# Sketched linear attention and an FFN in one kernel: squares on GpSimd, a paired x step and a new hand-written order

## The chip, the cores and the metric

The kernel runs on one core of a Trainium2 chip. The metric is the device time of one execution in microseconds (us), lower is better. Engines: PE is TensorE (PEld its weight loads), DVE is VectorE, ACT is ScalarE, POOL is GpSimd, SP is SyncE, which here only issues DMAs.

## What is computed

Two layers in a row, batch 4, 4 heads of 32, 1088 positions, d_model 128, d_ff 1024, everything given and returned in float32:

```python
def phi(x):                       # S1, S2: 8 x 32
    a = einsum('rd,bhsd->bhsr', S1, x)
    b = einsum('rd,bhsd->bhsr', S2, x)
    return outer(a, b)            # 64 features
q_p, k_p = phi(q), phi(k)
kv  = einsum('bhsf,bhsd->bhfd', k_p, v);  z = sum(k_p, axis=2)
x   = einsum('bhsf,bhfd->bhsd', q_p, kv) / (einsum('bhsf,bhf->bhs', q_p, z) + 1e-6)
# heads side by side: x is (4, 1088, 128)
x_prev = x shifted by one position, zero first
k   = relu((mu_k * x + (1 - mu_k) * x_prev) @ w_k)
out = sigmoid((mu_r * x + (1 - mu_r) * x_prev) @ w_r) * ((k * k) @ w_v)
```

## The kernel before

The 4352 positions are 34 tiles of 128. The attention part goes through them in ten groups of 2 or 4 tiles (QS), the FFN in ten groups of 1 to 4 (FS); k is done batch by batch, each in two groups of 4 and 5 tiles (KG). Loads come in on SP's DMA queue in the order k, v, q of batch 0, 1, 2, 3; the FFN weights come on POOL's queue, cast to bf16 on the way.

Each piece of work is a task with a name, and one long string, ORDER, gives the order in which the tasks are issued and the engine of each, `NAME/ENGINE`, for PE tasks also the PSUM bank (b0 to b7) that they open. There is no other scheduler: an engine does its tasks in that order and waits by semaphores for what they need. The names, with the number of the batch (K and XL, XF, XE) or the group behind them:

- KT transposes k (DVE), KP projects it with S1 and S2 (PE, into PSUM), KE copies the projections to SBUF, KF forms the 64 products per head (DVE, `outer`), KA accumulates k features times v and the sums needed for z (PE). KZ, KC, KD, KW, KB turn these into the block that q is multiplied with: KW puts the z part into SW, the joint projection weight, KB puts kv into kvS.
- QT transposes q, Q1 projects it with S1, S2 and z (PE), QE copies the z part w to SBUF, QP, QD, QI, QN compute the denominator, its reciprocal and the normalised factor (DVE), QF forms the products (DVE), QR transposes them (PE), QV copies them to SBUF, QX multiplies with kv (PE: the x step, in array tiles of 64 x 32, one per head).
- XP, XB, XL, XK (and XF, XE on POOL) make the two mixes of x and its shift in bf16; the last 32 and the first 32 positions of a batch take the way over XL.
- M1 is the first FFN matmul of one 128-wide chunk of d_ff, RE its ReLU out of PSUM, SQ the square of two chunks at once (SBUF to SBUF, bf16), M2 the second matmul, which accumulates over four SQ. RR and SG are the gate, FN multiplies by it and issues the output DMAs on SP's queue, four per group, or eight where the group crosses a batch.
- Z runs dummy matmuls on a tile of zeros.

In the order before, squares go to DVE (27) and ACT (13), ReLUs to ACT (66) and DVE (14), all 20 QV to ACT. POOL has the setup, the weight DMAs, XF and XE.

The helper `copy` is line 302 (ACT) and 304 (DVE) of the profile, `outer` is line 316, the x step 500, M1 541, ReLU 549 (ACT) and 551 (DVE), squares 558 (DVE) and 560 (ACT), M2 570, FN 595 and its DMAs 605, the q projection 440, the POOL pieces 526 to 533, the dummies 246.

Of the kernel before, what the change touches and what calls it, by code (L numbers as in the profile page):

```python
# [33 lines left out]
KF1_1_0/DVE QV1_1/ACT QX0/PE/b3 QV1_0/ACT QX1/PE/b4 XB0/ACT XL0/ACT XP0/ACT QD2/DVE XF0/POOL KA1_1_0/PE QT1_1/DVE
XP1/ACT XB1/ACT RR0/PE/b2 RR1/PE/b0 XK0/DVE SG0/ACT XK1/DVE SG1/ACT M10_4/PE/b3 M10_6/PE/b2 M10_1/PE/b5 M10_3/PE/b6
KZ1/DVE RE0_4/ACT QI2/DVE M10_7/PE/b0 M11_3/PE/b4 RE0_6/ACT KT2_1/DVE KC1/ACT M10_2/PE/b3 RE0_3/ACT RE1_3/ACT
KD1/PE/b7 RE0_2/ACT QN2/DVE RE0_1/ACT SQ0_1/DVE M11_6/PE/b3 M11_2/PE/b5 QF2_1/DVE KP2_1/PE/b4 KB1/ACT RE1_2/ACT
RE0_7/DVE M11_0/PE/b6 SQ1_1/ACT KW1/DVE M11_1/PE/b5 RE1_6/DVE M11_7/PE/b2 Q14/PE/b7 KE2_1/ACT SQ0_3/DVE QF2_0/DVE
RE1_7/ACT RE1_0/ACT M10_0/PE/b4 M10_5/PE/b3 Q13/PE/b0 KF2_1_0/DVE RE1_1/ACT RE0_5/ACT RE0_0/ACT SQ1_0/ACT QR2_0/PE/b3
QE3/ACT QR2_1/PE/b4 QE4/ACT SQ0_2/DVE QV2_0/ACT QP3/DVE M21_0/PE/b5 SQ0_0/DVE M21_1/PE QV2_1/ACT QD3/DVE M11_4/PE/b3  # L40
SQ1_3/DVE M11_5/PE/b6 M20_0/PE/b1 M20_1/PE RE1_4/ACT QI3/DVE M20_2/PE KT2_0/DVE M20_3/PE RE1_5/ACT QX2/PE/b4 SQ1_2/ACT
QN3/DVE FN0/DVE QF3_0/DVE KP2_0/PE/b6 XB2/ACT M21_2/PE QF3_1/DVE XP2/ACT M21_3/PE RR2/PE/b1 QP4/DVE KE2_0/ACT FN1/DVE
QR3_0/PE/b0 XK2/DVE SG2/ACT QR3_1/PE/b5 QV3_0/ACT QD4/DVE M12_6/PE/b4 KF2_0_0/DVE QV3_1/ACT M12_1/PE/b1 M12_0/PE/b0
M12_7/PE/b6 RE2_6/ACT QX3/PE/b5 RE2_0/ACT QI4/DVE QT2_1/DVE RE2_1/ACT M12_3/PE/b0 M12_2/PE/b4 XL1/ACT XP3/ACT QN4/DVE
KA2_0_0/PE/b1 XF1/POOL SQ2_0/DVE RE2_3/ACT M12_5/PE/b3 QF4_0/DVE XE0/POOL KA2_1_0/PE RE2_2/ACT QF4_1/DVE M22_0/PE/b0
RE2_5/ACT KZ2/DVE M12_4/PE/b4 XB3/ACT KT3_0/DVE QR4_1/PE/b7 RE2_4/ACT QR4_0/PE/b3 KC2/DVE KT3_1/DVE QV4_1/ACT
RR3/PE/b1 QV4_0/ACT KP3_0/PE/b4 SQ2_2/DVE SG3/ACT KP3_1/PE/b7 XK3/DVE SQ2_1/ACT QX4/PE/b1 KE3_1/DVE RE2_7/ACT
KE3_0/DVE M22_1/PE KF3_1_0/DVE XP4/ACT M22_2/PE SQ2_3/ACT M13_3/PE/b6 M13_0/PE/b4 M13_6/PE/b7 XK4/DVE KD2/PE/b5
# [665 lines left out]
```

## Time and profile before

| what | value |
|---|---|
| median of 3 runs | 100.59 us (99.74 to 100.81) |
| the profiled execution's own time | 99.74 us |
| its span in the trace | 97.9 us |
| DVE, ACT, POOL busy | 81%, 71%, 13% of the span |
| PE matmuls busy | 85% of the span |
| share of DMA queue q1 (SP) | 35.8% of 16 engines' span |

The trace is of one execution, and the time outside the span, some 1.9 us, is start and end. Successive instructions of an engine overlap a little in such a trace, so the mean of one is some 0.08 us longer than the distance to the next. In rows with `<-`, what stands behind it ended the idle time of the engine.

### The profile page before, as it was taken

To read this page: it belongs to the slowest core of one execution; us is meant where nothing else is said; L and a number is where in the kernel's file an instruction comes from. 1 tells how busy PE (TensorE), PEld (TensorE's weight loads), DVE (VectorE), ACT (ScalarE), POOL (GpSimd) and SP (SyncE) were. 2 spreads that over 40 slices of the span, in tenths; PEclk is the share of its full clock that TensorE was granted. 3 is DMA by queue.
4 is the path that set the end of the run, shared out by engine and by line. 5 is a ranking of instruction groups with operands and counts; after the bars stand their busy time and mean duration, and the time that the engine had idled before them with its cause. 6 is when DMAs were issued, how large, how long until landed. Compare 5 with 4: busy or idle time off the path is not lost.

```text
span 97.9 us, 3150 instructions
## 1 busy us (share of the span) xinstructions
PE 83.0 (85%) x1272; PEld 56.9 (58%) x1282; DVE 79.5 (81%) x184; ACT 69.8 (71%) x166; POOL 12.7 (13%) x44
## 2 busy tenths in 40 slices
PE   4997878993899999899999999999999979997100
PEld 1354557651668584885686876935588546766000
DVE  3189959997594989989999999997999989997200
ACT  3250023476667899999999996999999979997000
POOL 7280031020000002400000002200353001000000
PEclk9999999999859999999999999999999999999975
DMA  2799999999993012000022012022000241011351
GB/s 64 248 224 331 279 250 335 233 246 340 171 198 79 12 27 54 7 0 0 0 60 60 0 40 67 7 59 48 0 0 20 67 107 30 0 32 32 81 120 44
DMA packets 10063, 9.72 MB, mean 99 GB/s; under 512 B 2480, under 2 KB 8880, under 8 KB 10048
## 3 DMA queue, kind: packets, MB, share of 16 engines
q1 hardware_dynamic: 8528, 8.92, 35.8%
q0 software_dynamic: 1216, 0.59, 4.3%
q8 instruction: 10, 0.16, 0.7%
q14 instruction: 5, 0.04, 0.2%
q10 hardware_dynamic: 304, 0.00, 0.2%
HBM read 7.80 MB, written 2.23 MB: 102 GB/s over the span
## 4 chain that ended last, share of the span: by engine, by line
PE 60%; DMA 13%; ACT 9%; DVE 8%; issue 3%
PE ps_o L570 14%; DMA hdk<-in_k_dram 13%; PE ps_h L541 13%; PE ps_x L500 8%; PE ps_abw L440 6%; PE ps_qtp L485 6%; PE ps_kab L333 4%; PE ps_kv L361 3%; ACT k L549 3%; PE ps_r L582 3%; DVE kp L316 3%; ACT k L560 3%; PE ps_r L583 2%; ACT r L588 1%; DVE qp L316 1%
## 5 line engine op out<-in xcount | busy, mean ns | idle before, releaser
L549 ACT ACTIVATE k<-ps_h 128x512 bf16<-128x512 f32 (+3 forms) x66 | 31.7, 568 | 2.9 <-PE ps_h L541 2.7
L541 PE MATMUL ps_h<-XK,wk 128*128 128x512 bf16 (+3 forms) x72 | 19.1, 351 | 2.4 <-issue 2.0
L570 PE MATMUL ps_o<-wv,k 128*128 128x128 bf16 x272 | 19.0, 219 | 0.8 <-ACT k L560 0.6
L570 PEld LDWEIGHTS <-k 128*128 128x128 bf16 x272 | 16.5, 98 | 4.7 <-ACT k L549 0.8
L558 DVE TENSOR_TENSOR k<-k 128x1024 bf16<-128x1024 bf16 (+3 forms) x27 | 15.9, 606 | 2.8 <-ACT k L549 2.7
L560 ACT ACTIVATE k<-k 128x1024 bf16<-128x1024 bf16 (+2 forms) x13 | 12.1, 951 | 0.1
L316 DVE TENSOR_TENSOR qp<-an,ps_abw 128x512 f32<-128x512 f32 x17 | 11.2, 678 | 0.0
L316 DVE TENSOR_TENSOR kp<-ab 128x512 f32<-128x512 f32 (+3 forms) x10 | 10.9, 1111 | 0.1
L541 PEld LDWEIGHTS <-wk 128*128 128x128 bf16 x80 | 6.5, 98 | 6.7 <-issue 4.2
L302 ACT COPY qpT<-ps_qtp 128x512 f32<-128x512 f32 (+1 forms) x20 | 9.9, 538 | 0.6 <-PE ps_qtp L485 0.3
L485 PE MATMUL ps_qtp<-ident,qp 128*128 128x128 f32 x68 | 9.6, 277 | 0.2 <-DVE qp L316 0.2
L500 PE MATMUL ps_x<-qpT,kvS 64*32 64x512 f32 (+7 forms) x104 | 9.3, 451 | 0.1
L526 POOL TENSOR_SCALAR PP<-XL,omu_k 128x31 f32<-128x31 f32 x4 | 2.0, 497 | 51.2 <-ACT XL L302 51.2
L485 PEld LDWEIGHTS ps_qtp<-ident,qp 128*128 128x128 f32 x68 | 7.5, 140 | 1.5 <-DVE qp L316 0.5
L551 DVE TENSOR_SCALAR k<-ps_h 128x512 bf16<-128x512 f32 (+3 forms) x14 | 8.3, 608 | 0.1
L440 PE MATMUL ps_abw<-SW,qT 128*64 128x96 f32 x136 | 8.3, 266 | 0.0
L246 PE MATMUL wt<-zero 128*128 128x512 bf16 x19 | 6.9, 515 | 1.6 <-DVE warm L155 1.2
L440 PEld LDWEIGHTS ps_abw<-SW,qT 128*64 128x64 f32 x136 | 6.6, 147 | 2.3 <-DVE pw L456 0.6
L595 DVE TENSOR_TENSOR osb<-ps_o,r 128x512 f32<-128x512 f32 (+3 forms) x10 | 6.0, 602 | 1.4 <-PE ps_o L570 1.4
L361 PE MATMUL ps_kv<-kp,vt 128*32 128x64 f32 x288 | 5.6, 222 | 1.6 <-DVE kp L316 1.2
L326 DVE STREAM_TRANSPOSE kT<-hdk 128x256 f32<-128x256 f32 (+1 forms) x16 | 6.1, 427 | 1.1 <-DMA hdk<-in_k_dram 1.0
L361 PEld LDWEIGHTS ps_kv<-kp,vt 128*32 128x32 f32 x288 | 4.5, 110 | 4.0 <-DVE kp L316 1.9
(77 smaller groups left out, 110.9 us busy)
## 6 DMA issues: line engine op xcount, KB each, us to landing
hdk<-in_k_dram SPq DMA_DIRECT2D x4, 544.0 KB, 10.0
hdq<-in_q_dram SPq DMA_DIRECT2D x4, 544.0 KB, 11.5
vt<-in_v_dram SPq DMA_DIRECT2D x4, 288.0 KB, 9.8
vt<-in_v_dram SPq DMA_DIRECT2D x4, 256.0 KB, 9.9
out_dram<-osb SPq DMA_DIRECT2D x16, 64.0 KB, 1.8
out_dram<-osb SPq DMA_DIRECT2D x20, 32.0 KB, 1.6
out_dram<-osb SPq DMA_DIRECT2D x8, 48.0 KB, 1.6
wk<-in_moe_w_k_dram POOLq DMA_DIRECT2D x1, 256.0 KB, 8.9
```

The lines of the kernel that those rows point to most:

```text
L302: nc.scalar.copy(o, i)
L316: nc.vector.tensor_mul(o.rearrange("p t h i j -> p (t h) i j"), _ap(a_, [[sa, y], [1, R], [0, R]]), _ap(b_, [[sb, y], [0, R], [1, R]]))
L361: nc.tensor.matmul(kv[32 * h:32 * h + 32, :64], vt[b][:, h, T, :], kp[:, t, h].rearrange("p i j -> p (i j)"), start=(T == 0), stop=(T == 8 ...
L440: nc.tensor.matmul(p[64 * c:64 * c + 64, t * 96:t * 96 + 96], qT[:, s:s + 64], SW[:, s // S].rearrange("p h x r -> p (h x r)"), skip_group ...
L485: nc.tensor.transpose(p[:, t * P:t * P + P], qp[g][:, t, 2 * pair:2 * pair + 2].rearrange("p h i j -> p (h i j)"), ident[:])
L500: nc.tensor.matmul(p[D * h:D * h + D, c0:c0 + m], kvS[r:r + 64, b, D * h:D * h + D], qpT[g][r:r + 64, h // 2, c0:c0 + m], skip_group_check ...
L541: nc.tensor.matmul(h[:, :n * P], wk[:, c * P:(c + 1) * P], XK[:, F0[g] * P:(F0[g] + n) * P])
L549: nc.scalar.activation(o, i, RELU)
L551: nc.vector.tensor_scalar(o, i, 0.0, None, op0=mybir.AluOpType.max)
L558: nc.vector.tensor_mul(k2[:, :, :n * P], k1[:, :, :n * P], k1[:, :, :n * P])
L560: nc.scalar.activation(k2[:, :, :n * P], k1[:, :, :n * P], mybir.ActivationFunctionType.Square)
L570: nc.tensor.matmul(o[:, t * P:t * P + P], k2s[g, j][:, c, t * P:t * P + P], wv[:, w * j + c, :], start=(j == 0 and c == 0 and t == 0), sto ...
```

## The change

The tasks stay the same in kind; their code, their engines and their order change.

- SQ goes to POOL (20) and ACT (17); only three squares of the last FFN group stay on DVE. ReLUs are now 55 on ACT and 25 on DVE, QV 14 and 6, QE 4 and 6, KE 6 and 2.
- KF reads one factor of the product straight from the PSUM bank of KP; the other still comes from the SBUF copy. The bank is therefore held until KF is done.
- QX is issued once for two groups (QY only opens the bank of the earlier one). For odd groups the heads of the features are rotated by one, by a copy of head 0 behind head 3 in SW, so that the two groups' eight matmuls stand in eight different array tiles.
- Q1 projects whole tiles of 128 positions, and splits only those that cross a batch.
- w_v is loaded with eight consecutive rows per partition, 4 KB in a run; the columns of w_k are permuted to match by a new task, WKP, on ACT. w_r is loaded on SP's queue behind q of batch 0 instead of POOL's.
- The zero tile is fp32 and the dummies are 3 at the start and 1 later, instead of 12 and 9.
- In ORDER, q of group 0 is now done before k of batch 1.

The diff without the ORDER string but for its first line, and without a task's cost figures, which nothing reads:

```diff
-KT0_0/DVE S4T/PE/b0 KT0_1/DVE S4E/ACT KP0_0/PE/b1 KE0_0/DVE KP0_1/PE/b0 KF0_0_1/DVE KE0_1/DVE KF0_0_0/DVE KF0_1_1/DVE
+KT0_0/DVE S4T/PE/b0 KT0_1/DVE S4E/ACT KP0_0/PE/b1 KE0_0/ACT KP0_1/PE/b0 KF0_0_1/DVE KE0_1/ACT KF0_0_0/DVE KF0_1_0/DVE
...
-    zero = const.tile([P, 512], BF16)
+    zero = const.tile([P, P], F32)
...
     load_q(0, nc.sync)
+    nc.sync.dma_start(wr_f[:], moe_w_r)
...
-    wk = const.tile([P, DFF], BF16)
+    wkn = const.tile([P, DFF], BF16)
+    wk = const.tile([P, NC, P], BF16)
...
-    nc.gpsimd.dma_start(wk[:], moe_w_k)
-    nc.gpsimd.dma_start(wr_f[:], moe_w_r)
-    nc.gpsimd.dma_start(wv[:], moe_w_v.rearrange("(c p) d -> p c d", p=P))
+    nc.gpsimd.dma_start(wkn[:], moe_w_k)
+    nc.gpsimd.dma_start(wv[:], moe_w_v.rearrange("(p c) d -> p c d", p=P))
...
-    SW = const.tile([FD, B, H, 3, R], F32)
+    SW = const.tile([FD, B, H + 1, 3, R], F32)
...
-            nc.tensor.matmul(wt[:], zero[:, :P], zero[:], skip_group_check=True)
+            nc.tensor.matmul(wt[:], zero[:], _ap(zero[:], [[0, 4], [1, P]]), skip_group_check=True)
 
-    dummy(12)
+    dummy(3)
...
+    nc.vector.tensor_copy(SW[:D, 0, H, :2, :], St[:, :, :R])
...
+    def wk_perm(eng):
+        o, i = wk[:].rearrange("p c f -> p f c"), wkn[:].rearrange("p (f c) -> p f c", c=NC)
+        if eng == "ACT":
+            nc.scalar.copy(o, i)
+        else:
+            nc.gpsimd.tensor_copy(o, i)
...
     def k_feat(b, gi, t0, t1):
-        a_, b_ = ab[:, 1, t0:t1], ab[:, 0, t0:t1]
-        outer(kp[:, t0:t1], a_, b_)
+        n = KG[gi][1] - KG[gi][0]
+        a_ = tiles[f"kab_{b}_{gi}"][:, :n * 64].rearrange("p (t h x r) -> p t h x r", h=H, x=2, r=R)[:, t0:t1, :, 1]
+        outer(kp[:, t0:t1], a_, ab[:, 0, t0:t1])
...
     def k_w(b, eng):
-        copy(eng, SW[:, b, :, 2, :], tiles[f"kf_{b}"][:, :HR].rearrange("p (h r) -> p h r", h=H))
+        w = tiles[f"kf_{b}"][:, :HR].rearrange("p (h r) -> p h r", h=H)
+        copy(eng, SW[:, b, :H, 2, :], w)
+        copy(eng, SW[:, b, H, 2, :], w[:, 0])
...
     def q_proj(g):
         p = bank(f"abw_{g}")
         for t in range(QS[g]):
-            for c in range(2):
-                s = (Q0[g] + t) * P + 64 * c
-                nc.tensor.matmul(p[64 * c:64 * c + 64, t * 96:t * 96 + 96], qT[:, s:s + 64],
-                                 SW[:, s // S].rearrange("p h x r -> p (h x r)"),
-                                 skip_group_check=True, tile_position=(0, 64 * c))
+            s = (Q0[g] + t) * P
+            whole = s // S == (s + P - 1) // S
+            for lo, hi in [(0, P)] if whole else [(0, 64), (64, P)]:
+                kw = {} if whole else dict(tile_position=(0, lo))
+                nc.tensor.matmul(p[lo:hi, t * 96:t * 96 + 96], qT[:, s + lo:s + hi],
+                                 SW[:, (s + lo) // S, g % 2:g % 2 + H].rearrange("p h x r -> p (h x r)"), skip_group_check=True, **kw)
...
-    def q_x(g):
-        p = bank(f"x_{g}")
-        for b, c0, s, m in qsegs(g):
-            for h in range(H):
-                r = 64 * (h % 2)
-                nc.tensor.matmul(p[D * h:D * h + D, c0:c0 + m], kvS[r:r + 64, b, D * h:D * h + D],
-                                 qpT[g][r:r + 64, h // 2, c0:c0 + m], skip_group_check=True, tile_position=(r, D * h))
+    def q_x(pair):
+
+        jobs = []
+        for i, g in enumerate(pair):
+            if i:
+                bank(f"x_{g}")
+            for n, (b, c0, s, m) in enumerate(qsegs(g)):
+                for y in range(H):
+                    h, r = (y + g % 2) % H, 64 * (y % 2)
+                    jobs.append((n, y, g, b, c0, m, h, r))
+        for n, y, g, b, c0, m, h, r in sorted(jobs):
+            nc.tensor.matmul(tiles[f"x_{g}"][D * h:D * h + D, c0:c0 + m], kvS[r:r + 64, b, D * h:D * h + D],
+                             qpT[g][r:r + 64, y // 2, c0:c0 + m], skip_group_check=True, tile_position=(r, D * h))
...
-    nc.tensor.matmul(h[:, :n * P], wk[:, c * P:(c + 1) * P], XK[:, F0[g] * P:(F0[g] + n) * P])
+    nc.tensor.matmul(h[:, :n * P], wk[:, c], XK[:, F0[g] * P:(F0[g] + n) * P])
...
     def sq(g, j, eng):
-        if eng == "DVE":
-            nc.vector.tensor_mul(k2[:, :, :n * P], k1[:, :, :n * P], k1[:, :, :n * P])
+        if eng != "ACT":
+            (nc.vector if eng == "DVE" else nc.gpsimd).tensor_mul(k2[:, :, :n * P], k1[:, :, :n * P], k1[:, :, :n * P])
```

How the new order moves instructions, at three places. A row is line, operation, output<-inputs and shape, in the order in which the engine does them. First the end of DVE: `k<-ps_h` is a ReLU, `k<-k` a square, `osb<-ps_o,r` is FN, here of the groups 7, 8 and 9. Before:

```order
L558 TENSOR_TENSOR k_1680<-k_1652 128x1024
L595 TENSOR_TENSOR osb<-ps_o,r 128x512
L558 TENSOR_TENSOR k_1711<-k_1630 128x1024
L558 TENSOR_TENSOR k_1721<-k_1687 128x1024
L551 TENSOR_SCALAR k_1723<-ps_h 128x384
L551 TENSOR_SCALAR k_1746<-ps_h 128x384
L551 TENSOR_SCALAR k_1717<-ps_h 128x384
L595 TENSOR_TENSOR osb<-ps_o,r 128x512
L558 TENSOR_TENSOR k_1775<-k_1717 128x2x384
L595 TENSOR_TENSOR osb<-ps_o,r 128x384
```

Now, also the end of DVE, with the last group's squares:

```order
L572 TENSOR_SCALAR k_1653<-ps_h 128x384
L572 TENSOR_SCALAR k_1631<-ps_h 128x384
L572 TENSOR_SCALAR k_1653<-ps_h 128x384
L579 TENSOR_TENSOR k_1685<-k_1639 128x2x384
L579 TENSOR_TENSOR k_1697<-k_1653 128x2x384
L616 TENSOR_TENSOR osb<-ps_o,r 128x512
L579 TENSOR_TENSOR k_1733<-k_1683 128x2x384
L616 TENSOR_TENSOR osb<-ps_o,r 128x512
L616 TENSOR_TENSOR osb<-ps_o,r 128x384
```

FN7 stood eight instructions ahead of FN9; it now stands three ahead of it, behind two of the last group's squares.

The end of POOL, XF and XE of the last batches, before (XL and PP are pieces of the x mix):

```order
L526 TENSOR_SCALAR PP<-XL,omu_k 128x31
L527 CAST XB<-XL 128x31
L528 CAST XB<-XL 128x32
L532 TENSOR_SCALAR XL<-XL,mu_k 128x32
L533 TENSOR_TENSOR XK<-XL,PP 128x32
L532 TENSOR_SCALAR XL<-XL,mu_k 128x32
L533 TENSOR_TENSOR XK<-XL,PP 128x32
```

Now, the same end of POOL:

```order
L579 TENSOR_TENSOR k_1398<-k_1221 128x1024
L579 TENSOR_TENSOR k_1453<-k_1363 128x1024
L579 TENSOR_TENSOR k_1513<-k_1449 128x1024
L579 TENSOR_TENSOR k_1540<-k_1468 128x1024
L553 TENSOR_SCALAR XL<-XL,mu_k 128x32
L554 TENSOR_TENSOR XK<-XL,PP 128x32
L579 TENSOR_TENSOR k_1606<-k_1580 128x1024
L579 TENSOR_TENSOR k_1651<-k_1608 128x1024
```

Full-size squares now stand in front of XE of the last batch and behind it, the last two being those of FFN group 8.

PE at the x step of the groups 0 and 1, before (ps_qtp are the transposes QR, ps_kv is KA; the numbers tell buffers apart):

```order
L485 MATMUL ps_qtp_386<-ident_110,qp_372 128x128 x2
L485 MATMUL ps_qtp_391<-ident_110,qp_372 128x128 x2
L500 MATMUL ps_x_398<-qpT_384,kvS_132 32x256 x4
L500 MATMUL ps_x_404<-qpT_396,kvS_132 32x256 x4
L361 MATMUL ps_kv_330<-kp_394,vt1_81 32x64 x20
```

Now, at the same step on PE, the first rows of eight that go on in turn:

```order
L500 MATMUL ps_qtp_348<-ident_112,qp_339 128x128 x2
L373 MATMUL ps_kv_356<-kp_341,vt1_81 32x64 x16
L379 MATMUL ps_kv_356<-ab_325 32x32 x4
L521 MATMUL ps_x_322<-qpT_310,kvS_134 32x256
L521 MATMUL ps_x_377<-qpT_351,kvS_134 32x256
```

The matmuls of two groups, into two PSUM banks, alternate where one group's four came after the other's.

More of the change, by code (lines that the diff above doesn't have):

```diff
@@ L34 @@
[L34 to L48, printed above, removed]
```

110 lines of the change are left out of this document (69 added, 41 removed).

## The prediction

> **What bounds the kernel now.** I read the busy times by stage first, cut where the kind of work changes, then who waits for whom, then the end of the program, the DMA queue included. By stage (busy us and, in brackets, instructions of each engine, then the granted clock, DMA share and GB/s):
>
> ```profile
> 0.00:4.60 4.60, 3.37 (x8) 1.16 (x9) 0.96 (x6) 1.49 (x2) 1.93 (x18) 1.00 0.51 154
> 4.60:24.00 19.40, 15.60 (x339) 10.31 (x340) 17.55 (x46) 7.35 (x30) 4.47 (x11) 1.00 1.10 280
> 24.00:34.00 10.00, 9.06 (x114) 6.61 (x115) 7.11 (x20) 6.92 (x20) 0.00 (x0) 0.83 0.66 120
> 34.00:84.00 50.00, 48.62 (x740) 34.04 (x745) 47.46 (x102) 48.00 (x104) 6.33 (x17) 1.00 0.14 32
> 84.00:91.54 7.54, 6.30 (x82) 4.80 (x80) 6.41 (x12) 6.04 (x12) 0.00 (x0) 1.00 0.13 29
> 91.54:97.90 6.36, 0.00 (x0) 0.00 (x0) 0.00 (x0) 0.00 (x0) 0.00 (x0) 0.72 0.35 84
> sum 97.90, PE 82.95 PEld 56.92 DVE 79.50 ACT 69.80 POOL 12.73; mean PE 13.82 PEld 9.49 DVE 13.25 ACT 11.63 POOL 2.12
> ```
>
> The reader is to see three things. From 34 to 84 us PE, DVE and ACT are all busy for 47 to 49 of 50 us, so taking work from one alone gives little there. DVE is full from the first k on: up to 91.54, where its last instruction ends, it works 79.5 us and idles 12.0 (3.6, 1.9, 2.9, 2.5 and 1.1 by stage). POOL idles. The 2.9 us between 24 and 34 have a cause of their own; the chain of waits and the list of waits show it:
>
> ```profile
> 23.60 1.34 issue
> ```
> ```profile
> PE ps_h L541 <- issue: 2.0, 1, 2.0
> DVE kT L326 <- DMA hdk<-in_k_dram: 1.0, 1, 1.0
> ```
>
> PE stands 2.0 us at the first FFN matmuls with nothing to wait for, and in the same stage its clock is 0.83. The end belongs to the queue that issues the output. Timeline of DVE, then two windows of SP:
>
> ```profile
> 85.62 0.68 DVE L595 TENSOR_TENSOR osb<-ps_o,r 128x512 f32<-128x512 f32 x1
> 88.84 0.68 DVE L595 TENSOR_TENSOR osb<-ps_o,r 128x512 f32<-128x512 f32 x1
> 89.44 0.55 DVE L558 TENSOR_TENSOR k<-k 128x768 bf16<-128x768 bf16 x1
> 90.98 0.56 DVE L595 TENSOR_TENSOR osb<-ps_o,r 128x384 f32<-128x384 f32 x1 [0.99 <-PE ps_o L570]
> ```
> ```profile
> 86.33 9.32 SPq L605 DMA_DIRECT2D out_dram<-osb  x16
> ```
> ```profile
> 91.63 1.82 SPq L605 DMA_DIRECT2D out_dram<-osb  x4
> ```
>
> FN7 ends at 86.30, and from 86.33 SP issues the 16 output DMAs of FN7 (8), FN8 (4) and FN9 (4) without a break until 95.65; FN9 has been done since 91.54. An issue costs 0.455 us undisturbed (1.82/4), 0.58 over the sixteen. The span ends 2.25 us after the last issue. So the end hangs on FN7 more than on FN9.
>
> **The change, part by part.** Rows by shape (busy us, then mean ns of one), the first four over all shapes:
>
> ```profile
> L549 ACT ACTIVATE k<-ps_h 128x512 bf16<-128x512 f32 (+3 forms) x66 | 31.7, 568 | 2.9 <-PE ps_h L541 2.7
> L558 DVE TENSOR_TENSOR k<-k 128x1024 bf16<-128x1024 bf16 (+3 forms) x27 | 15.9, 606 | 2.8 <-ACT k L549 2.7
> L560 ACT ACTIVATE k<-k 128x1024 bf16<-128x1024 bf16 (+2 forms) x13 | 12.1, 951 | 0.1
> L551 DVE TENSOR_SCALAR k<-ps_h 128x512 bf16<-128x512 f32 (+3 forms) x14 | 8.3, 608 | 0.1
> ```
> ```profile
> L302 ACT COPY qpT<-ps_qtp 128x512 f32<-128x512 f32 x14 | 8.0, 606 | 0.3
> L560 ACT ACTIVATE k<-k 128x1024 bf16<-128x1024 bf16 x7 | 7.5, 1075 | 0.0
> L316 DVE TENSOR_TENSOR qp<-an,ps_abw 128x512 f32<-128x512 f32 x17 | 11.2, 678 | 0.0
> L316 DVE TENSOR_TENSOR kp<-ab 128x512 f32<-128x512 f32 x3 | 2.0, 686 | 0.0
> L304 DVE CAST XB<-ps_x 128x512 bf16<-128x512 f32 x1 | 0.7, 692 | 0.6 <-ACT PP L509 0.6
> L304 DVE COPY ab<-ps_kab 128x256 f32<-128x256 f32 x3 | 1.3, 421 | 0.5 <-PE ps_kab L333 0.4
> L304 DVE COPY wsb<-ps_abw 128x128 f32<-128x128 f32 x1 | 0.3, 291 | 0.1
> ```
>
> *DVE.* Of 27 squares three of 768 columns stay: -(15.9 - 3 x 0.55) = -14.2. ReLUs rise from 14 to 25 and from 6144 to 11392 columns (counted in the two orders): +5248 x 8.3/6144 = +7.1. Six copies of transposed features come over: 5 x 0.69 + 0.42 = +3.9. Four more copies of w at 0.2 to 0.3: +1.0. Three k evacuations leave: -1.3. One XP, one small XB, three XL come, one KB goes, 0.2 to 0.75 each: +1.5. Sum -2.0 us, bounds -1.4 and -2.7 (successive DVE rows overlap by some 0.08 us, so any count is that uncertain per instruction).
>
> *ACT.* ReLU columns 28672 to 23424: -5.8. Squares 11008 to 15104 columns: +4.5. Six copies of features -3.4, four of w -1.0, k evacuations +1.2, the rest of the x step and k copies -0.8, the weight permutation +1.1 (the 1024-column row; its stride of 8 is not in the trace, bounds 0.9 and 2.2). Sum -4.2. The permutation waits for the w_k DMA and holds QE2 and QV0 behind it; the first FFN matmul that needs it comes some 8 us later. I take 0 on the path, 0.5 at most.
>
> *POOL.* It gets 20 squares, 17408 columns, 17 full-size ones. Rows of POOL, whole list, then one line's view with min/median/max, then a timeline of both engines:
>
> ```profile
> L532 POOL TENSOR_SCALAR XL<-XL,mu_k 128x32 f32<-128x32 f32 x4 | 1.5, 369 | 0.0
> L229 POOL TENSOR_SCALAR wr_c<-wr_f,mu_r 128x128 bf16<-128x128 f32 x1 | 0.6, 594 | 0.0
> ```
> ```profile
> L527 POOL CAST XB<-XL x4: 213/217/740, 21.0 to 70.5; 128x31 bf16<-128x31 f32 x4
> ```
> ```profile
> 70.50 1.30 DVE L558 TENSOR_TENSOR k<-k 128x1024 bf16<-128x1024 bf16 x2
> 70.51 0.74 POOL L527 CAST XB<-XL 128x31 bf16<-128x31 f32 x1
> 71.19 0.67 POOL L528 CAST XB<-XL 128x32 bf16<-128x32 f32 x1
> ```
>
> No POOL row is this wide. Lower bound: DVE's 0.68 us a square; upper: 369 ns for 32 columns in proportion, 11.8 us. The slope between the two POOL rows is (594-369)/96 = 2.34 ns a column, so 0.37 + 992 x 0.00234 = 2.7 us; I take that, as the slope is the nearest thing to a rate. POOL then has 17 x 2.7 + 6.3 (its work after 24) = 52 us, in about 60 us between the first ReLU pair and the last FFN output: off the path, though not by much. The Trainium skill, GPSIMD Engine Reference, section 3.1, states about 2.6 cycles an element for two inputs at 1.2 GHz, and section 4.1 advises VectorE for elementwise work as about twice as fast: an estimate of 2.2 us a square, and POOL at 44 us; no run here shows it yet.
>
> The casts that met DVE's squares took 0.74 and 0.67 us instead of 0.21, as long as the DVE square itself: a DVE instruction with both inputs in SBUF shuts POOL out. The k products were the other such kind (kp<-ab); reading one factor from PSUM costs nothing (678 against 686 ns) and keeps POOL free, at the price of a PSUM bank held about 1.2 us longer (0 to 0.5, taken as 0: there are eight).
>
> *PE.* Chain rows and the x group:
>
> ```profile
> 36.96 1.07 PE ps_x L500 x16
> 43.85 1.04 PE ps_x L500 x8
> 57.88 0.81 PE ps_abw L440 x16
> ```
> ```profile
> L500 PE MATMUL ps_x<-qpT,kvS 64*32 64x512 f32 (+7 forms) x104 | 9.3, 451 | 0.1
> ```
>
> A step of four array tiles takes 1.04 us for 512 columns; ten steps 9.3. If eight tiles run together, five steps cost 4 x 1.04 + 0.6 = 4.8: -4.5. If tiles in one column of the array take turns, 0; no row shows two such. I take -4, as the four tiles of today, two to a row half, overlap fully (eight 512-column passes in 1.04 us). The price is that the earlier group of a pair waits for the later. The q projection goes from 0.81/4 us a tile to two whole-array passes: 0 to -1, taken as 0.
>
> *At no cost.* The wr load is one more SP issue (64 KB, about 0.25 us at 280 GB/s) ahead of the next k; DVE now does q of group 0 before that k, which covers it and the old 1.0 us wait. wv in 4 KB runs lands earlier, but its first use is at 31 us. POOL issues one DMA fewer. Fewer and wider dummies: DVE sets the pace before 24 us (17.6 of 19.4), so 0; without that cover, a half-rate stretch like that of 24 to 34 us, 1.7 us. The k copies on ACT and KW0 on DVE add two waits of 0.4 to 0.7 us on DVE early, with the q work queued behind; they replace the 1.0 us wait for k: 0, bounds -1.0 and +1.2.
>
> *Sum.* DVE's last instruction: work -2.0. Idle at 24 to 34: the 2.9 falls to about 1.4, since the order there is another and half of it was PE's pause (bounds 0 and -2.9): -1.5. Idle after 34, 3.7 us: ACT and PE leave DVE waiting a little less: -0.8 (0 and -1.5). So FN9 ends 4.3 us earlier, at 87.2.
>
> The end, however, gets longer. On DVE FN7 now stands after the squares of the last group; between its end and FN9's are one square, FN8 and FN9: 0.55 + 0.68 + 0.56 = 1.8 us, where there were 5.2. All 16 issues follow FN7, so the span ends at FN9 - 1.8 + 16 x (0.455 to 0.58) + 2.25, that is 7.7 to 9.7 us behind FN9, where it was 6.36: +1.4 to +3.4. I take +2.0, nearer the undisturbed issue.
>
> Net -4.3 + 2.0 = -2.3 us. The profiled execution took 99.74 us, span 97.9; it was the fastest of three, 0.85 below the median of 100.59. The same step from the median: 98.3.
>
> **The rivals.** (A) The tail doesn't grow, because POOL or PE hands FN7 over in time or issues go at 0.455, and PE's pause at 24 us goes altogether: another -2.3, 96.0. For it: the pause waits for nothing that the profile names. Against: FN7's place in the order.
>
> (B) POOL shuts DVE out as DVE now shuts out POOL. At the very end POOL does its last two squares back to back just as DVE comes to its three squares from SBUF, ahead of FN7. If DVE must let the running one finish, some 1.6 us of 2.7, FN7 and all 16 issues shift: 99.9. The rows above show only POOL losing; POOL's pieces were too short to show the other. The Trainium skill, SBUF — State Buffer, section "Who interferes with whom", says that whoever issues first gets the shared pair for the whole instruction; its half that the rows show, they confirm.
>
> (C) Slower: POOL becomes the bound. It decides from (60 - 6.3)/17 = 3.2 us a square; each 0.1 us above adds 1.7. At 3.4 us POOL needs 64 us, FN9 ends 4.1 later: 102.4. For it: a two-input instruction may cost more than the one-input slope that I used, and XF, XE and the M2 groups queue behind squares in order. By the skill's estimate of 2.2 us, above, C would not happen.
>
> (D) The eight tiles take turns: the PE gain is gone, PE bounds 34 to 84 us as before, only the 1.5 us at 24 us stay, against a tail of +2.0: 101.1.
>
> **How the numbers follow.** Mine 0.42 (own range 97.0 to 99.8; 0.39 of it faster), A 0.17, B 0.20 (0.05 faster, 0.15 same), C 0.13, D 0.08 (0.06 same, 0.02 slower). About 1% is what a measurement of this kernel tells from no change. Faster 0.39 + 0.17 + 0.05 = 0.61; same 0.03 + 0.15 + 0.06 = 0.24; slower 0.13 + 0.02 = 0.15. The range leaves out most of C and the best part of A: 95.2 to 101.2.
>
> **What would show it.** POOL squares near 2.7 us (2.2 by the page; above 3.2 C). An x step over two groups near 1.04 us (2 us: D). DVE busy near 77.5 and done near 87. SP issuing 16 DMAs without a break from FN7 on, over 7.3 us long, and the span ending 8 us or so behind FN9 (6.4: A). A DVE square of the last group far over 0.55 us, or late beside a POOL square: B. Wrong altogether if DVE idles over 13 us: then the new order, and not the engines' sums, sets the time.

## The result, and the profile after

| | before | after |
|---|---|---|
| median of all runs (us) | 100.06 (48 runs) | 98.98 (43 runs) |
| profiled execution: own time, span (us) | 99.74, 97.9 | 98.58, 96.6 |
| FN7 ends, FN9 ends (us) | 86.30, 91.54 | 86.45, 88.10 |
| span end behind FN9 (us) | 6.36 | 8.50 |

The ratio after to before is 1.000, 95% interval 0.997 to 1.003: no difference that can be measured, where a gain of 2.3 us had been forecast. The ratio, like the medians in the table of experiments below, leaves out executions over 1.5% above the fastest of their kernel, and that matters here: of 59 runs of before beside the experiments the eleven with a granted clock (the mean share of full speed at which TensorE ran) of 0.975 or more have a median of 98.07 us, the 32 from 0.962 to 0.975 one of 99.78 and the 16 below one of 100.92, while the changed kernel shows 98.80 at 0.96 or more, 98.78 from 0.9425 to 0.96 and 99.42 below.

The changed kernel by stage, cut as before up to 84 us and then at the end of FN9 (busy us and instructions of PE, PEld, DVE, ACT, POOL, then clock, DMA share, GB/s):

```profile
0.00:4.60 4.60, 3.50 (x5) 1.61 (x6) 1.09 (x7) 1.49 (x2) 1.76 (x16) 1.00 0.55 152
4.60:24.00 19.40, 15.78 (x311) 11.63 (x309) 15.62 (x43) 11.38 (x25) 3.23 (x8) 0.82 1.03 279
24.00:34.00 10.00, 9.85 (x173) 8.11 (x172) 9.96 (x26) 8.48 (x29) 2.84 (x7) 1.00 0.57 129
34.00:84.00 50.00, 48.08 (x674) 34.87 (x665) 46.43 (x104) 45.92 (x92) 33.51 (x33) 1.00 0.15 31
84.00:88.10 4.10, 3.51 (x60) 3.18 (x57) 4.10 (x8) 2.28 (x5) 0.88 (x1) 1.00 0.08 16
88.10:96.60 8.50, 0.00 (x0) 0.00 (x0) 0.00 (x1) 0.00 (x0) 0.00 (x0) 0.77 0.38 78
sum 96.60, PE 80.72 PEld 59.41 DVE 77.20 ACT 69.55 POOL 42.22; mean PE 13.45 PEld 9.90 DVE 12.87 ACT 11.59 POOL 7.04
```

DVE works 77.2 us instead of 79.5, as forecast. Its idle time up to FN9 is 10.9 us instead of 12.0: 3.5, 3.8, 0.0, 3.6 and 0.0 by stage, where it was 3.6, 1.9, 2.9, 2.5 and 1.1. So the stage from 24 to 34 us gave 2.9, and the one before it took 1.9 back. The stretch in which TensorE runs at half its clock, here called the half rate, has moved too: the clock is 0.82 from 4.6 to 24 us and full from 24 to 34. Then the end, timeline of DVE and of SP:

```profile
84.82 1.03 DVE L579 TENSOR_TENSOR k<-k 128x768 bf16<-128x768 bf16 x2
85.76 0.69 DVE L616 TENSOR_TENSOR osb<-ps_o,r 128x512 f32<-128x512 f32 x1
86.38 0.56 DVE L579 TENSOR_TENSOR k<-k 128x768 bf16<-128x768 bf16 x1
86.86 1.24 DVE L616 TENSOR_TENSOR osb<-ps_o,r 128x512 f32<-128x512 f32 x2
```
```profile
86.48 7.75 SPq L626 DMA_DIRECT2D out_dram<-osb  x16
```

FN9 ends 3.4 us earlier, but FN7, which stands in front of all 16 last DMAs, ends where it did (86.45, was 86.30). SP then issues for 7.75 us without a break, 0.48 each. The prediction says the same of the profile before, but there the fourth of the 16 took 1.80 us, where all but one of the others took 0.3 to 0.45:

```profile
87.64 1.80 SPq L605 DMA_DIRECT2D out_dram<-osb  x1
```

With FN7 at the same place, that one issue is most of the 1.3 us by which the two spans differ (97.9 and 96.6). Rows that had been priced, by shape, and one step of the chain of waits:

```profile
L579 POOL TENSOR_TENSOR k<-k 128x1024 bf16<-128x1024 bf16 x16 | 30.1, 1892 | 12.3 <-ACT k L570 10.2 <-DVE k L572 1.9
L281 ACT COPY wk<-wkn 128x1024 bf16<-128x1024 bf16 x1 | 4.8, 4768 | 0.4 <-DMA wkn<-in_moe_w_k_dram 0.4
L456 PE MATMUL ps_abw<-SW,qT 128*128 128x96 f32 x64 | 9.5, 290 | 0.6 <-DVE SW L315 0.6
```
```profile
33.48 1.02 PE ps_x L521 x17
```

A POOL square takes 1.89 us, the permutation of w_k 4.77, an x step of two groups 1.02.

### The profile page after: what moved, and what is told of

It reads as the page before. It is cut to its first block, busy times and chain, and to the rows that moved or that the text cites. A ratio compares the mean times of both kernels' runs of the same rounds, so it can differ in the third digit from the quotient of the medians.

```text
span 96.6 us, 3021 instructions
## 1 busy us (share of the span) xinstructions
PE 80.7 (84%) x1199; PEld 59.4 (61%) x1205; DVE 77.2 (80%) x185; ACT 69.5 (72%) x151; POOL 42.2 (44%) x63
## 4 chain that ended last, share of the span: by engine, by line
PE 53%; DVE 18%; DMA 8%; ACT 5%; SPq 4%; issue 2%; ACTq 0%
PE ps_o L591 12%; PE ps_h L562 10%; DMA vt<-in_v_dram 7%; PE ps_qtp L500 6%; PE ps_abw L456 6%; PE ps_kv L373 5%; PE ps_kab L344 4%; PE ps_x L521 4%; DVE XK L534 4%; DVE kT L337 3%; DVE k L572 3%; SPq L626 3%; PE ps_r L603 2%; DVE qp L327 2%; DMA out_dram<-osb 1%
## 5 line engine op out<-in xcount | busy, mean ns | idle before, releaser
L579 POOL TENSOR_TENSOR k<-k 128x1024 bf16<-128x1024 bf16 (+1 forms) x20 | 32.5, 1636 | 14.6 <-ACT k L570 12.5
L570 ACT ACTIVATE k<-ps_h 128x512 bf16<-128x512 f32 (+3 forms) x55 | 25.7, 541 | 1.3 <-PE ps_h L562 1.1
L572 DVE TENSOR_SCALAR k<-ps_h 128x512 bf16<-128x512 f32 (+2 forms) x25 | 14.4, 623 | 0.1
L327 DVE TENSOR_TENSOR kp<-ps_kab,ab 128x512 f32<-128x512 f32 (+3 forms) x10 | 10.9, 1112 | 1.2 <-ACT ab L313 1.2
L456 PE MATMUL ps_abw<-SW,qT 128*128 128x96 f32 (+1 forms) x72 | 10.2, 288 | 0.6 <-DVE SW L315 0.6
L456 PEld LDWEIGHTS ps_abw<-SW,qT 128*128 128x128 f32 (+1 forms) x72 | 8.8, 191 | 2.1 <-DVE SW L315 0.8
L534 DVE SCALAR_TENSOR_TENSOR XK<-ps_x,mu_k,PP 128x512 bf16<-128x512 f32 (+8 forms) x13 | 6.7, 536 | 0.7 <-ACT XB L313 0.7
L344 PE MATMUL ps_kab<-SW,kT 128*64 128x64 f32 x144 | 6.7, 250 | 0.2 <-ACT qpT L313 0.2
L344 PEld LDWEIGHTS ps_kab<-SW,kT 128*64 128x64 f32 x144 | 5.6, 159 | 1.4 <-ACT qpT L313 0.4
L603 PE MATMUL ps_r<-wr_c,XB 128*128 128x128 bf16 (+1 forms) x36 | 5.3, 224 | 1.4 <-ACT XB L313 0.9
```

Source lines behind the costliest of these rows:

```text
L327: nc.vector.tensor_mul(o.rearrange("p t h i j -> p (t h) i j"), _ap(a_, [[sa, y], [1, R], [0, R]]), _ap(b_, [[sb, y], [0, R], [1, R]]))
L344: nc.tensor.matmul(p[64 * c:64 * c + 64, (t - t0) * 64:(t - t0) * 64 + 64], kT[b][:, t, 64 * c:64 * c + 64], SW[:, 0, :H, :2, :], skip_gro ...
L456: nc.tensor.matmul(p[lo:hi, t * 96:t * 96 + 96], qT[:, s + lo:s + hi], SW[:, (s + lo) // S, g % 2:g % 2 + H].rearrange("p h x r -> p (h x ...
L534: nc.vector.scalar_tensor_tensor(XK[:, b * S + s:b * S + s + m], tiles[f"x_{g}"][:, c0:c0 + m], mu_k[:], PP[:, b * XW + s:b * XW + s + m], ...
L570: nc.scalar.activation(o, i, RELU)
L572: nc.vector.tensor_scalar(o, i, 0.0, None, op0=mybir.AluOpType.max)
```

## The experiments

Three theories went in. *Queue*: the change did win time, but the end hangs on FN7 and the 16 issues behind it. *Start*: the gain is lost before 27 us. *Chance*: the profile of before held accidents. Each kernel is one edit of before, of after, or of an earlier experiment. They were measured in four groups of rows (four, four, four and three). The ratio is to runs of before taken with the group; that base moves (its median is 99.5, 98.0 and 99.3 us in the first three groups, and the kernel before against itself gave 0.986), so the kernels' own medians are the better guide from group to group. By the same median after has 98.78 us. The last three kernels have no ratio.

| kernel | median us (runs kept, of all) | ratio, 95% | FN7, FN9 end | span |
|---|---|---|---|---|
| before_again | 98.19 (2 of 4) | 0.986 (0.976 to 0.996) | 86.94, 92.17 | 98.2 |
| after_fn7 | 97.02 (4 of 6) | 0.975 (0.967 to 0.982) | 84.87, 88.87 | 95.1 |
| after_2q | 95.71 (4 of 6) | 0.960 (0.954 to 0.967) | 86.91, 88.56 | 93.8 |
| before_2q | 96.26 (3 of 6) | 0.967 (0.959 to 0.974) | 84.96, 90.20 | 93.8 |
| after_both | 95.12 (5 of 6) | 0.976 (0.966 to 0.985) | 84.55, 88.56 | 93.0 |
| both_x1 | 97.68 (6 of 10) | 0.999 (0.989 to 1.009) | 87.85, 91.86 | 96.3 |
| both_q64 | 97.00 (5 of 10) | 0.991 (0.984 to 0.998) | 86.22, 90.23 | 96.0 |
| b2q_pool | 108.16 (4 of 4) | 1.109 (1.095 to 1.124) | 95.98, 102.58 | 106.2 |
| both_wkpool | 94.87 (5 of 6) | 0.956 (0.950 to 0.963) | 85.01, 89.02 | 93.5 |
| both_wundo | 94.85 (5 of 6) | 0.957 (0.952 to 0.962) | 84.56, 88.57 | 93.1 |
| both_kpsb | 97.32 (4 of 4) | 0.981 (0.975 to 0.988) | 86.66, 90.66 | 95.2 |
| before_late3 | 96.14 (3 of 4) | 0.969 (0.962 to 0.975) | 87.30, 92.53 | 96.4 |
| wundo_ke | 95.04 (4 of 6) | | 84.69, 88.69 | 93.2 |
| both_dummies | 95.56 (6 of 6) | | 85.17, 89.17 | 93.6 |
| both_sqdve | 102.26 (4 of 4) | | 92.14, 96.14 | 100.6 |

**before_again.** No edit.

> The kernel before, unchanged. Three theories of why the changed kernel gained nothing. Queue: FN9 does end earlier (88.10 against 91.54 us in the two profiles), but the end hangs on FN7, which ends at 86.45 now and 86.30 before, followed by 16 output DMAs at 0.47 us each and 2.4 us. Start: the gain is lost before 27 us, where DVE now idles 3.7 instead of 1.9 us (5.6 and 4.6 to 24) and the FFN begins 4 us later. Chance: the first profile of before held stalls that other executions do not have (PE's pause of 2.0 us at 23.6, TensorE at half rate for 3.4 us, two breaks of 1.4 and 0.45 us in SP's issues after FN7). Queue expects FN7 to end within 0.5 us of 86.3 again and the span to end 16 x 0.47 + 2.4 = 9.9 us behind it (96.2) if no issue is broken. Chance expects DVE's idle time between 24 and 34 us to fall from 2.9 to 1.5 us or less, and FN7 at 85 or before. Start expects the idle time as it was, 12.0 us to FN9. The ratio to before must be 1.00.

DVE's busy time from 24 to 34 us is 6.54 us here, and 7.98 in before_2q, whose clock was full all the time (third column of busy times):

```profile
24.00:34.00 10.00, 8.37 (x100) 5.98 (x99) 6.54 (x19) 6.54 (x19) 0.00 (x0) 0.83 0.52 111
```
```profile
24.00:34.00 10.00, 8.92 (x135) 6.82 (x135) 7.98 (x23) 7.91 (x23) 0.00 (x0) 1.00 0.62 128
```

The idle time of DVE there is 3.5 us (2.9 in the first profile) and still 2.0 in before_2q, so this stall is no accident. FN7 ends 0.6 us later than in the first profile and SP's 16 issues took 8.7 us, again with a long one (1.23 us), so the span is 98.2 and not 96.2. PE's pause at the first FFN matmul is there every time: 2.0 us in the first profile, 2.6 in this one, 2.3 in before_2q. The half rate near 26 us is there in two of the three, and FN9 ends at 91.54 and 92.17 with it, at 90.20 without. Chance is right for the half rate alone.

**after_fn7.** FN7 and the matmuls that it needs, moved ahead:

```diff
-... RE9_3/DVE M28_0/PE/b3 RE9_5/DVE M28_1/PE RE9_1/ACT RE9_2/DVE M27_3/PE RE9_6/ACT
+... RE9_3/DVE M27_3/PE FN7/DVE M28_0/PE/b3 RE9_5/DVE M28_1/PE RE9_1/ACT RE9_2/DVE RE9_6/ACT
-... RE9_7/ACT FN7/DVE M28_3/PE
+... RE9_7/ACT M28_3/PE
```

> The changed kernel with M2 of FFN group 7's last piece and FN7 put some ten tasks earlier in the order; nothing else. POOL's last square of group 7 ends at 79.4 us, so FN7 can end near 83.2 instead of 86.45. Queue: FN7's 8 DMAs are then issued by 87, FN8 (87.5) and FN9 (88.15) follow without a queue in front of them, the last issue ends near 91.3, the span near 93.7: 2.9 us less than the changed kernel (ratio to before 0.97). Start and chance: the end follows FN9, which does not move: within 0.5 us of the changed kernel (ratio 0.995 to 1.005).

```profile
84.18 0.69 DVE L616 TENSOR_TENSOR osb<-ps_o,r 128x512 f32<-128x512 f32 x1 [0.21 <-PE ps_o L591]
```
```profile
84.90 7.83 SPq L626 DMA_DIRECT2D out_dram<-osb  x16
```

FN7 ends 1.6 us earlier, the span 1.5 us, although FN9 ends 0.8 us later than in after: the end follows FN7. By medians it is 1.8 us, less than the 2.9 expected: FN7 ends at 84.87, not at 83.2.

**after_2q and before_2q.** In after every second DMA of the groups 7 to 9 goes to ACT's queue; in before, where ACT still works behind FN7, those of FN8 and half of FN9's:

```diff
-                nc.sync.dma_start(orow[b][:, x:x + 4 * m - 3:4, :], o[32 * y:32 * y + 32, t:t + m, :])
+                eng = nc.scalar if g > 6 and y % 2 else nc.sync
+                eng.dma_start(orow[b][:, x:x + 4 * m - 3:4, :], o[32 * y:32 * y + 32, t:t + m, :])
```
```diff
+                eng = nc.scalar if g == 8 or g == 9 and y % 2 else nc.sync
+                eng.dma_start(orow[b][:, x:x + 4 * m - 3:4, :], o[32 * y:32 * y + 32, t:t + m, :])
...
-RE9_6/DVE FN8/DVE SQ9_2/ACT
+RE9_6/DVE SQ9_2/ACT FN8/DVE
```

> The changed kernel with every second output DMA of FN7, FN8 and FN9 issued on ACT's queue, which is done with its work at 86.3 us. Queue: eight issues on each queue from 86.5, done at 90.2, span end 92.6 instead of 96.6: 4 us less (ratio to before 0.96). If the moving of the bytes and not the issuing sets the end, nothing changes. Start and chance: under 1 us, since the issuing would not be what ate the gain.

> The kernel before with FN8's four output DMAs on ACT's queue (behind ACT's last square, 90.04 us) and FN9's four shared by both queues; FN7's eight stay on SP, since ACT still works then. Queue: the end hangs on FN9 here (91.54 + 0.94 + 2.3 = 94.8 to 95.1 us) instead of 96.2 to 97.9, a ratio of 0.97 to 0.99; and the changed kernel with two queues must be 2 to 2.5 us faster than this one, because with the queue out of the way FN9's 3.4 us show. Start and chance: the two kernels with two queues differ by under 1 us, as the two kernels with one do.

SP in after_2q, then in before_2q:

```profile
86.94 3.67 SPq L627 DMA_DIRECT2D out_dram<-osb  x8
```
```profile
84.99 6.04 SPq L606 DMA_DIRECT2D out_dram<-osb  x10
```

Both are some 3 us faster than their originals (98.78 to 95.71, and a ratio of 0.967): the issuing set the end in both. With one queue FN7 alone counts, and FN7 had not moved. But after_2q beats before_2q by 0.6 us, not by the 2 to 2.5 that Queue expected and within the 1 us that Start and Chance allowed: if the tail hid a gain, it was far smaller than thought. In after_2q all 16 issues still stand behind FN7, so the next kernel moves that too.

**after_both.** after_fn7 with FN8's DMAs and one of FN9's on ACT's queue (`g == 8 or g == 9 and y == 3`).

> The changed kernel with FN7 early (as in the run with FN7 alone moved) and both queues: FN7's eight DMAs on SP, FN8's four on ACT, FN9's four 3 to 1. Queue theory: FN7 ends near 84.9, its issues are through at 88.6, FN9 ends near 88.8, the last issue 1.4 us later and the span 2.4 after that: 92.6, so 1.2 us less than the changed kernel with two queues alone (93.8), ratio to before near 0.95. If the queue had no part left in the end: 93.8 again, 0.96. Full forecast: FN9 earlier by 4.3 us than in before would mean FN9 at 87.2 and 91.0 us; the profiles so far have it at 88.1 to 88.9, against 90.3 to 92.2 in before.

```profile
83.86 0.69 DVE L616 TENSOR_TENSOR osb<-ps_o,r 128x512 f32<-128x512 f32 x1 [0.21 <-PE ps_o L591]
88.00 0.56 DVE L616 TENSOR_TENSOR osb<-ps_o,r 128x384 f32<-128x384 f32 x1 [0.31 <-PE ps_o L591]
```
```profile
84.58 5.29 SPq L627 DMA_DIRECT2D out_dram<-osb  x11
```
```profile
87.72 2.39 ACTq L627 DMA_DIRECT2D out_dram<-osb  x5
```

The last issues, on SP and on ACT (second and third fence), are now FN9's, and the span ends 4.4 us behind FN9. 95.12 us is 3.7 less than after, and 1.1 less than before_2q, whose end is FN9's too. FN9 ends 1.6 us earlier than in before_2q, but its issue on ACT waits behind FN8's four, and the spans differ by 0.8 (93.0 and 93.8). So the change is worth 1.6 us at FN9 and 0.8 to 1.1 us of time where FN7 doesn't stand in front of it, against the 4.3 of the forecast at FN9.

**both_x1.** The x step one group at a time: `QY` becomes `QX` in the order, and

```diff
-        two = (g - 1, g) if g % 2 else (g,)
+        two = (g,)
```

> The kernel after_both with the x step undone: one group at a time, four matmuls in four array tiles, at the place in the order where the group's bank was opened; the heads stay rotated. If the eight tiles saved PE time on the path: PE busy rises by 4 us (x groups near 1.04 us for 512 columns each, ten instead of five) and the time by 1 to 4 us. If PE only waits less somewhere else: PE busy +4 us, time within 0.5 us, since DVE sets FN9. If the early bank and the wait for the later group cost more than the pair saves: 0.5 to 1 us faster.

The x step in the stretch from 0 to 90 us, both_x1 and then after_both (PE first):

```profile
0.00:90.00 90.00, 8.72 (x104) 2.04 (x104) 9.80 (x21) 8.51 (x22) 0.96 0.41 101
```
```profile
0.00:90.00 90.00, 5.03 (x104) 1.53 (x104) 9.87 (x21) 8.55 (x22) 1.00 0.43 105
```

3.7 us of PE, a little of it by the half rate that both_x1's profile had from 12.8 to 19.6 us, and 2.6 us of time: the eight tiles run together, and PE's time is on the path.

**both_q64.** The q projection in tiles of 64 positions again (`for lo, hi in [(0, 64), (64, P)]`).

> The kernel after_both with the q projection in tiles of 64 positions again (68 matmuls of 128 x 64 weights instead of whole ones). In the profiles a group of four took 0.81 us before and 1.02 to 1.06 now, 8 x 0.2 us of PE. If that is on the path, 0.5 to 1.6 us faster, and the first groups' waits of DVE for the projection (0.7 us before the copy of w) shrink by 0.2 us each; if DVE sets the pace, within 0.3 us of after_both, with PE busy 1.6 to 2 us less.

```profile
PE ps_abw L456 <- issue: 1.4, 1, 1.4
```

Slower by 1.9 us, against both expectations. PE's 705th instruction (matmuls, weight loads and semaphore waits, as the trace records them) now is a q projection, and PE stands 1.4 us in front of it; in after_both it is a k projection, 0.2. DVE idles 1.5 us behind it, TensorE works at half rate from 26.1 to 29.5, and FN9 ends 1.7 us later. Whole tiles are slower by themselves (8 in 1.02 us, where 16 took 0.81), but they are half as many instructions. How much of the 1.9 us is the pause's and how much the half rate's, the profile doesn't tell; both_dummies, below, has as many more instructions ahead of that place, a pause of 1.0 us and no half rate, and costs 0.4.

**b2q_pool.** before_2q with 18 of DVE's squares on POOL, nothing else.

> The kernel before with two queues (before_2q), and 18 of DVE's 27 squares (FFN groups 1 to 7) put on POOL at the same places of the order; ReLUs, QV and all else stay, and k products still have both inputs in SBUF. DVE loses 18 x 0.6 = 10.8 us of work. If DVE's work sets the end, FN9 is several us earlier. If ACT and PE set it too, as the busy times say (PE 48.6, ACT 48.0 of 50 us), little comes of it: DVE idles up to 10 us more and the time moves by less than 1.5 us; where M2 waits for a POOL square of 1.9 us in an order made for one of 0.6 us, it gets slower by 1 to 3 us. On the shared port: if a DVE instruction with two SBUF inputs holds POOL, POOL squares beside k products or DVE squares take up to 1.5 us longer than 1.89; if POOL holds DVE as well, k products of 0.69 us take up to 2 us longer.

Squares on POOL and on DVE (min, median, max ns), then a wait of PE:

```profile
L558 POOL TENSOR_TENSOR k<-k x18: 1893/1895/2341, 27.1 to 91.3; 128x1024 bf16<-128x1024 bf16 x17, 128x512 bf16<-128x512 bf16 x1
L558 DVE TENSOR_TENSOR k<-k x9: 280/580/2240, 24.6 to 100.5; 128x256 bf16<-128x256 bf16 x4, 128x1024 bf16<-128x1024 bf16 x4, 128x768 bf16<-128x768 bf16 x1
```
```profile
PE ps_o L570 <- POOL k L558: 7.3, 5, 2.6
```

11.9 us slower than before_2q: in the old order PE waits 7.3 us for POOL. And where DVE and POOL squares met, near 91.5 us, POOL's took 2.34 us and DVE's 2.24 instead of 0.68: either shuts the other out.

**both_wkpool and both_wundo.** The permutation on POOL (`WKP/POOL`), and no permutation at all:

```diff
-    nc.gpsimd.dma_start(wkn[:], moe_w_k)
-    nc.gpsimd.dma_start(wv[:], moe_w_v.rearrange("(p c) d -> p c d", p=P))
+    nc.gpsimd.dma_start(wk[:], moe_w_k)
+    nc.gpsimd.dma_start(wv[:], moe_w_v.rearrange("(c p) d -> p c d", p=P))
```

> The kernel after_both with the permutation of w_k on POOL instead of ACT; nothing else. In the profiles it holds ACT from 12.9 to 17.7 us (4.77 us; it had been priced at 1.1), with QE2, the first QV and the first KE of batch 1 behind it, and the first FFN matmul comes at 25.1 to 25.8 us instead of 22.3 to 22.9. Theory of the permutation: this is what gave the gain back; off ACT, DVE's wait of 0.7 us at 17 goes, the FFN begins 2 us or more earlier and the time falls by 1 to 2 us (span 91 to 92, ratio to after_both 0.98 to 0.99). Rival: DVE is full in that stretch anyway (idle 0.7 of 9 us), so FN9 moves by 0.7 us at most, and a POOL copy that holds DVE out can even cost 1 us.

> The kernel after_both with the weights loaded as before: w_v with rows p, 128 + p and so on, 256 bytes in a run, w_k as it is, no permutation at all. Theory of the permutation: as for POOL, 1 to 2 us faster than after_both, without a copy that could hold DVE. Rival: 0 to 0.7 us faster from DVE's wait; and if the long runs of w_v matter, its landing (10.0 us after issue now, 16.5 before) makes the first M2 wait, near 30 us, and the time rises.

```profile
L283 POOL COPY wk<-wkn x1: 4762/4762/4762, 13.0 to 13.0; 128x1024 bf16<-128x1024 bf16 x1
```
```profile
PE ps_kab L335 <- issue: 1.0, 1, 1.0
```

Each 0.3 us faster, which is within what can be told apart from group to group: the permutation is not what cost the start. In both_wundo (second fence) DVE's wait at 17 us is gone and the FFN begins 0.7 us earlier, but then PE stands 1.0 us in front of its 705th instruction, and FN9 ends where it did.

**both_kpsb.** Both factors of the k products from SBUF.

> The kernel after_both with both factors of the k products from the SBUF copy again. In the run with squares on POOL alone a DVE square that met a POOL square took 2.24 us instead of 0.68, and the POOL one 2.34 instead of 1.89: each shuts the other out. Here six k products of batches 2 and 3 (0.69 to 1.49 us) fall into POOL's time, from 26 us on. If the lock is what the PSUM read avoids: one or two of them take up to 1.9 us longer, POOL squares up to 1.5, and the time rises by 0.5 to 2 us. If not: within 0.3 us.

DVE of both_kpsb, DVE of after_both:

```profile
40.62 3.06 DVE L327 TENSOR_TENSOR kp<-ab 128x1280 f32<-128x1280 f32 x1
```
```profile
39.65 1.48 DVE L327 TENSOR_TENSOR kp<-ps_kab,ab 128x1280 f32<-128x1280 f32 x1
```

One product meets a POOL square (40.45 to 42.35) and takes 3.06 us instead of 1.48; DVE works 1.5 us more in all and idles 0.6 us more, FN9 ends 2.1 us later, and the time rises by 2.2.

**before_late3.** before_2q with the loads of batch 3 issued in FN0.

> The kernel before with two queues (before_2q), and the loads of batch 3 issued behind FN0's output instead of at the start. In all profiles of before PE stands 2.0 to 2.6 us at its 703rd instruction (matmuls and weight loads counted), the first FFN matmul, 256 behind its 447th where it also stands up to 0.9 us; in the changed kernel the same place comes at 27.2 us and costs 0.0 to 0.7. Theory: every 256 instructions PE needs a block of code, fetched by the DMA engines behind the loads, 8 us at 17 to 25 us. Then with a quarter of the loads gone until 34 us the pause at the 703rd shrinks to under 1 us, the FFN begins 1.5 to 2 us earlier and the time falls by 1 to 2 us. Rival: the pause belongs to the first FFN matmul and stays 2.0 to 2.6.

```profile
PE ps_h L541 <- issue: 2.6, 1, 2.6
```

The pause stays 2.6 us, at the same 703rd instruction, with a quarter of the loads out of the way (TensorE is at half rate from 26.5 us on in this profile, hence FN9 at 92.53). The median doesn't move either (96.14, before_2q 96.26). That it waits behind the loads is not borne out.

**wundo_ke, both_dummies, both_sqdve.** both_wundo with KE0 on DVE, KW0, QE0 and QE1 on ACT; after_both with the old dummies; after_both with the 20 POOL squares on DVE.

> The kernel both_wundo (no permutation of w_k) with the copies of batch 0's k projections (KE0) back on DVE as before, and KW0, QE0, QE1 on ACT as before. Theory of the start's waits: DVE loses some 0.9 us of idle time before 15 us (k copies on ACT made it wait 1.0 instead of 0.4 us, KW0 and QE0 0.47 and 0.71), the FFN begins earlier and FN9 ends 0.5 to 1 us before both_wundo's 88.57. Theory of the wall: PE passes its 705th instruction at 26.9 us again (after_both 26.93, both_wundo 26.95), stands longer in front of it, and FN9 stays within 0.3 us of 88.57.

> The kernel after_both with the dummies of before: bf16, 12 at the start and 5, 2 and 2 later instead of 3 fp32 ones and 1. That is 17 more matmuls and 17 more weight loads ahead of the FFN. The forecast priced the dummies at 0, and 1.7 us if TensorE then ran at half rate where it is not covered. If the dummies matter for the clock: no stretch at half rate before 24 us, and 0.2 to 0.5 us faster than after_both. If the fixed count of instructions matters: PE's 705th instruction now comes some 34 instructions earlier in the program, in the q projection of group 3 or the first FFN matmuls, its pause there is 1 to 2 us instead of 0.2, and the time rises by 0.5 to 1.5 us, as in both_q64 where 34 more instructions stood ahead of it.

> The kernel after_both with its 20 squares on POOL put on DVE, at the same places of the order; ReLUs stay. DVE gets 16 x 0.6 + 4 x 0.25 = 10.6 us more work. If DVE's work sets FN9: 9 to 11 us slower than after_both (ratio 1.10). If the waits for POOL (a square of 1.89 us where DVE takes 0.68) cost PE and DVE much, some is won back: 5 to 8 us slower. The forecast's price of the squares with what went the other way (14.2 us off DVE, 13 us of other work on it) needs the first.

PE in both_dummies:

```profile
PE ps_h L562 <- issue: 1.0, 1, 1.0
```

wundo_ke changes nothing (95.04, both_wundo 94.85), and there is no less idle time: DVE now waits 1.5 us in one place, for QE0 on ACT. PE goes on at 27.07 us. In both_dummies PE's pause is at its 703rd instruction, now an FFN matmul; it goes on at 26.80, and the time rises by 0.4. In both_sqdve DVE works 9.4 us more (86.7), and 7.1 us of them show, so some is won back, but most of the squares' price is real.

## Why the prediction was wrong

**The sums of DVE and PE: right.** DVE -2.0 was forecast, -2.3 came. The x step was to save PE 4 us; it went from 9.31 to 5.03 in the two first profiles, and undoing it costs 2.6 us. ACT was to lose 4.2 and lost 0.25, because the permutation takes 4.77 us and not 1.1 (its upper bound was 2.2); that size was wrong, its 0 on the path was right (both_wundo). POOL's square takes 1.89 us, below the 2.7 taken, and there are 16 full-size ones and not 17, so that C never came near, and D fell with the x step. The 2.2 us estimated from the Trainium skill, GPSIMD Engine Reference, section 3.1, is nearer, but above the 1.89 too. Of A the half came true that PE's pause goes.

**The tail: right in size.** +2.0 was forecast and +2.1 came, by the way that was named: FN7 did not move, all 16 issues follow it, 8.5 us from FN9 to the end where 7.7 to 9.7 were worked out. after_fn7 and after_2q show that it is this. What the forecast did not draw from it: if the end hangs on FN7 in both kernels, a gain at FN9 counts only as far as it moves FN7. By the forecast's own sum FN7 was to end at 87.2 - 1.8 = 85.4; it ended at 86.45, where it had been at 86.30.

**The idle time: the step that failed.** The sum took -1.5 from 24 to 34 us, -0.8 after 34 and 0 (bounds -1.0 and +1.2) for the start. In the profiles it is -2.9, -0.1 and +1.8: -1.1 in all, where -2.3 had been summed up. So FN9 came 3.4 us earlier and not 4.3, and the two profiles differ by 1.3 us of span and not 2.3. The waits at the start, list of waits of after:

```profile
DVE kp L327 <- ACT ab L313: 1.2, 2, 1.0
DVE wsb L315 <- PE ps_abw L456: 1.0, 2, 0.7
DVE pw L471 <- ACT wsb L313: 0.9, 2, 0.7
DVE SW L315 <- ACT kvS L313: 0.5, 1, 0.5
```

The longest of each (last column) all fall before 18 us and come to 2.9 us; they replace the 1.0 us wait for k and one of 0.4 for the first k projection. Two such waits had been counted, four came. They are also, as far as the runs show, why the stall from 24 to 34 us went: the FFN now begins 3.5 us later (25.8 us, was 22.3), and PE passes its 705th instruction at 27.2 with no pause, where it stood 2.0 us at the 703rd from 23 on. Start and stall hang together: without the permutation's wait the FFN begins 0.7 us earlier, and the pause in front of the 705th instruction grows from 0.2 to 1.0 us (both_wundo; 0.5 in wundo_ke). PE goes on there at 26.80 to 27.07 us in both_dummies, after_both, both_wundo and wundo_ke, but that is no fixed time: it is 26.15 in both_q64, 27.90 in both_kpsb and some 25 in the kernel before. What all 17 profiles have in common is a transfer of 16 KB on the instruction queue, which starts 2.5 to 2.9 us before PE goes past (3.4 in both_sqdve), whether PE has to stand or not. What sets its start is open.

**The base: the same step from the median.** The profile that was read had the half rate at 26.1 to 29.5 us, in the very stage whose idle time was to fall. The forecast didn't split it off, and took its step from the median of three executions, the profiled one among them. Without it before idles 2.0 us in that stage, not 2.9, and FN9 ends at 90.20 (before_2q). Against that FN9 gains 1.6 us in after_both, not 4.3: DVE's 2.1 us less work, and 0.4 us more idle time (11.4, was 10.9). With +2.1 us of tail on top nothing is left, which agrees with the ratio of 1.000. At FN7, on which the end hangs, after is even 1.5 us behind before_2q (86.45, 84.96), and before at a granted clock of 0.975 or more is 0.7 us ahead (98.07, 98.80). Where before does have the half rate, the changed kernel is ahead (99.78, 98.78), since its own, from 14.2 to 21.0 us in the profile, lies where it costs little.

**Rival B: the mechanism was right, the place wrong.** POOL does hold up a DVE instruction with two SBUF inputs, by 1.6 us as worked out (k product 3.06 instead of 1.48, DVE square 2.24 instead of 0.68). At the end of the changed kernel it doesn't show, as DVE's squares there take 0.56 us: POOL's last square is over at 84.88, just as DVE's first begins (84.82). That the k products read PSUM was priced at 0 for their duration, which is right; with POOL's squares it is worth 2.2 us (both_kpsb), most of it by that one product.

**The q projection: a missed term.** 0 was taken, 0 to -1 allowed. A group of four costs 0.2 us more on PE, but undoing it costs 1.9 us, and not through PE's time for them. The pause shows that their number matters; how much of the 1.9 us it is, beside the half rate, is open (0.4 in both_dummies).
